# Attention backward for one query per head: uneven K loads, larger stores, a coarser last V load

## The chip, the core and the metric

The kernel runs on one core of a Trainium2 chip. The core has a matrix engine (PE), a vector engine (DVE), a scalar engine (ACT), GpSimd (POOL) and a sync engine (SP) that issues transfers; the transfers themselves are carried by 16 DMA engines, which move rows between the device memory (HBM, "dram" in the profile) and the on-chip memory with its 128 partitions. The metric is device time in microseconds (us); less is better. The kernel before takes 668.13 us (median of 3 runs, 668.04 to 668.19).

## The reference, cut to what matters

There are 32 heads, one query row per head, 8192 keys and values of 128 numbers each, all bf16. What is computed is the attention output and the gradients of q, k and v for a given output gradient.

```python
B, H, Sq, Skv, Dh = 1, 32, 1, 8192, 128

def _fwd_reference(q, k, v):
    scale = q.shape[-1] ** -0.5
    scores = jnp.einsum('bhqd,bhkd->bhqk', q, k) * scale
    attn = _softmax(scores, axis=-1)
    return jnp.einsum('bhqk,bhkd->bhqd', attn, v)

def reference(q, k, v, grad_out):
    _out, _vjp = jax.vjp(_fwd_reference, q, k, v)
    return (_out, *_vjp(grad_out))          # out, dq, dk, dv
```

Per head, K and V are 2 MB each and are read once; dk and dv are 2 MB each and are written once. Since there is one query row, dk is the outer product of the score gradient (ds, 8192 numbers) with the q row, and dv the outer product of the probabilities (p) with the output-gradient row. Over 32 heads that is 134 MB in and 134 MB out.

## The kernel before: the parts that the change touches

Each head's 8192 rows are laid out as 128 partitions of NT = 64 consecutive rows ("slots") of 256 bytes, so that a partition's share of one head is 16 KB in one piece in HBM and on chip. A quarter of a head is CH = 16 slots per partition.

```python
CH = 16
R = 4
K_BUFS = 3
V_BUFS = 2
NST = 2
...
    NT = S // P              # 64 slots per partition
    NCH = NT // CH           # 4 quarters
...
    def rows_of(x, h, c, parts):
        L = NT // parts
        return x[0, h].rearrange("(p n) d -> p n d", p=P)[:, c * L:(c + 1) * L, :]

    def slots(X, c, parts):
        L = NT // parts
        return X[:, c * L:(c + 1) * L, :]

    def load_k(h):
        Kt[h] = kpool.tile([P, NT, D], BF16, tag="K", name="Kt")
        parts = NCH if h == 0 else 1
        for c in range(parts):
            nc.sync.dma_start(slots(Kt[h], c, parts), rows_of(k, h, c, parts))

    def load_v(h):
        Vt[h] = vpool.tile([P, NT, D], BF16, tag="V", name="Vt")
        parts = NCH if h in (0, H - 1) else 1
        for c in range(parts):
            nc.sync.dma_start(slots(Vt[h], c, parts), rows_of(v, h, c, parts))
```

A gradient tile G (dk or dv of one head) is written by DVE in four quarters, and sent out when enough quarters are done: with NST = 2 a store of 1 MB after every second quarter, and in the last head a store of 0.5 MB after each.

```python
    def outer(h, which, r):
        x = st[h]
        if r == 0:
            x[which] = gpool.tile([P, NT, D], BF16, tag=which, name="G_" + which)
        G, dst = x[which], out_2 if which == "dk" else out_3
        ...
        nc.vector.tensor_tensor(
            slots(G, r, 4).rearrange("p n (a b) -> p n a b", b=R), ..., op=ALU.mult)
        parts = 4 if h == H - 1 else NST
        if r % (4 // parts) == 4 // parts - 1:
            c = r // (4 // parts)
            nc.sync.dma_start(rows_of(dst, h, c, parts), slots(G, c, parts))
```

The loop over heads overlaps the scores of head h with the gradients of head h - 1. In each iteration the transfers are issued, all by SP and in this order:

```python
    for h in range(H + 1):
        p_ = h - 1
        if h < H:
            ...                                   # k_blocks x4 (DVE transposes), k_scores (PE)
            if 0 < h < H - 1:
                load_v(h + 1)
        if h > 0:
            ds_of(p_); outer(p_, "dk", 0); dq_of(p_, 0)
        ...
            dq_of(p_, 1); outer(p_, "dk", 1)      # store: first half of dk
        if 0 < h and h + 2 < H:
            load_k(h + 2)
        ...                                       # softmax of head h, outer(p_, "dk", 2)
        if h > 0:
            outer(p_, "dk", 3)                    # store: second half of dk
        if h == H:
            break
        ...                                       # p, v_transposes (PE, ACT), contract, v_scores
        outer(h, "dv", 0); outer(h, "dv", 1)      # store: first half of dv
        outer(h, "dv", 2); outer(h, "dv", 3)      # store: second half of dv
```

So one iteration issues six transfers: V (2 MB), half of dk (1 MB), K (2 MB), half of dk, and two halves of dv. The build gives the transfers eight completion semaphores in turn: a transfer is issued only when the one eight places before it has landed.

Of the kernel before, what the change touches and what calls it, by code (L numbers as in the profile page):

```python
# [16 lines left out]
R = 4  # L17
K_BUFS = 3
V_BUFS = 2
NST = 2  # L20
QD = 32


@with_exitstack
def kernel(
# [11 lines left out]
    nc = tc.nc  # L37
    P = 128
    _, H, S, D = k.shape
    assert D == P and S % (P * CH) == 0 and H <= P  # L40
    NT = S // P
    NCH = NT // CH
    NQ = P // QD
    assert NCH == 4 and NQ == 4
    W = D // 2
    NB = W // QD
    scale = float(D) ** -0.5
# [13 lines left out]
    Kt, Vt, XK, XV, st = {}, {}, {}, {}, {}  # L61
# [8 lines that stand above are left out]

    def load_k(h):
        Kt[h] = kpool.tile([P, NT, D], BF16, tag="K", name="Kt")
        parts = NCH if h == 0 else 1
        for c in range(parts):
            nc.sync.dma_start(slots(Kt[h], c, parts), rows_of(k, h, c, parts))

    def load_v(h):
        Vt[h] = vpool.tile([P, NT, D], BF16, tag="V", name="Vt")
        parts = NCH if h in (0, H - 1) else 1
        for c in range(parts):  # L80
            nc.sync.dma_start(slots(Vt[h], c, parts), rows_of(v, h, c, parts))

    rows = consts.tile([H, 2, D], BF16)
    nc.sync.dma_start(rows[:, 0, :], q.rearrange("b h s d -> (b h s) d"))
    nc.sync.dma_start(rows[:, 1, :], grad_out.rearrange("b h s d -> (b h s) d"))
    load_k(0)
    load_v(0)
    load_k(1)
    load_v(1)

    ident = consts.tile([P, P], BF16)
# [6 lines left out]
    nc.vector.reduce_sum(in_quad[:], ident[:].rearrange("p (a i) -> p a i", a=NQ), axis=AX.X)  # L98
    lane = consts.tile([P, QD], F32)
    nc.vector.reduce_sum(lane[:], ident[:].rearrange("p (a i) -> p i a", a=NQ), axis=AX.X)  # L100
# [3 lines left out]
    for w in range(NB):  # L104
        for e2 in range(2):
            four = consts.tile([H, NQ, QD], BF16, tag=f"four{w}{e2}")
            nc.vector.tensor_copy(
                four[:], rows[:, 0, :].rearrange("h (w j e) -> h w e j", w=NB, e=2)[:, w, e2:e2 + 1, :]
                .to_broadcast([H, NQ, QD]))
            tp = psT.tile([P, CH, P], BF16, tag="T")  # L110
# [17 lines left out]
    def k_blocks(h, u):  # L128


        if u == 0:
            XK[h] = ktpool.tile([P, CH, NB, NCH, QD], F32, tag="XK", name="XK_sb")
        nc.vector.transpose(XK[h][:, :, :, u, :],  # L133
# [54 lines left out]
# [5 lines that stand above are left out]
        rep, row = x["ds"] if which == "dk" else x["p"], x["qd"][:, 0 if which == "dk" else 1, :]  # L193
        Q = NT // 4
        nc.vector.tensor_tensor(  # L195
            slots(G, r, 4).rearrange("p n (a b) -> p n a b", b=R),
            slots(rep, r, 4).unsqueeze(2).to_broadcast([P, Q, D // R, R]),
            row.rearrange("p (a b) -> p a b", b=R).unsqueeze(1).to_broadcast([P, Q, D // R, R]),
            op=ALU.mult)
        parts = 4 if h == H - 1 else NST  # L200
        if r % (4 // parts) == 4 // parts - 1:
            c = r // (4 // parts)
            nc.sync.dma_start(rows_of(dst, h, c, parts), slots(G, c, parts))
# [24 lines left out]
# [3 lines that stand above are left out]
            x = st[h] = {}  # L231
            for u in range(NCH):
                k_blocks(h, u)
            k_scores(h)
# [3 lines that stand above are left out]
            ds_of(p_)  # L238
            outer(p_, "dk", 0)
            dq_of(p_, 0)  # L240
# [3 lines left out]
        if h > 0:  # L244
            dq_of(p_, 1)
            outer(p_, "dk", 1)
        if 0 < h and h + 2 < H:
            load_k(h + 2)
# [9 lines left out]
        if h > 0:  # L258
            outer(p_, "dk", 2)
# [77 lines left out]
```

## Time and profile before

| | before |
|---|---|
| time, median of 3 | 668.13 us |
| span of the profiled execution | 667.0 us |
| PE busy | 516.8 us (77%) |
| DVE busy | 512.5 us (77%) |
| ACT busy | 182.1 us (27%) |
| share of the 16 DMA engines' time, data transfers | 97.0% |
| share of the 16 DMA engines' time, instruction fetches | 0.7% |
| read and written | 134.23 MB and 134.23 MB, 403 GB/s over the span |

The profile is of one execution. A busy share is averaged over the whole span. The line of DMA digits divides the span in 40 slices, each digit the mean busy share of the 16 DMA engines in tenths (9 is 90% or more), and the line under it gives the GB/s moved in each slice. The chain "that ended last" follows the end of the program back from releaser to releaser. Under the page lies the trace, which holds a record for each packet that a DMA engine moved (start, duration in ns, bytes) and for each of the up to 16 semaphore counts by which the DMA engines report that their share of a transfer has landed. A packet record does not name its DMA engine.

### The profile page before, as it was taken

How to read it: one execution, taken by the hardware profiler on the slowest of the kernel's cores; microseconds unless marked ns; L12 is line 12 of the kernel's file. 1: busy time of each engine (PE TensorE's matmuls, PEld its weight loads, DVE VectorE, ACT ScalarE, POOL GpSimd, SP SyncE). 2: the span in 40 equal slices, each digit the busy share in tenths (PEclk: the TensorE clock that was granted, in tenths of full speed). 3: DMA queues.
4: the chain of work that ended last, by engine and by line, in shares of the span. 5: the costliest groups of instructions: out<-in, count | busy, mean ns of one | idle time of the engine just before them, and what ended most of it. 6: DMA issues, size and time to landing. Idle time of an engine off the chain costs nothing.

```text
span 667.0 us, 23105 instructions
## 1 busy us (share of the span) xinstructions
PE 516.8 (77%) x10727; PEld 485.8 (73%) x10727; DVE 512.5 (77%) x658; ACT 182.1 (27%) x321; POOL 0.7 (0%) x6
## 2 busy tenths in 40 slices
PE   2887988888887777878779787787776888778881
PEld 1887878878877767877668676677766777677870
DVE  4797888888877797777877778777788776887762
ACT  0333323232323222232222322223312223223230
POOL 0000000000000000000000000000000000000000
PEclk9995556566565565555555655666557665555555
DMA  8999999999999999999999999999999999999783
GB/s 330 414 425 424 419 427 414 424 423 426 425 425 424 425 425 424 425 429 423 423 427 426 423 416 422 413 412 418 395 423 418 397 416 406 409 420 403 270 357 142
DMA packets 29807, 269.94 MB, mean 405 GB/s; under 512 B 3472, under 2 KB 3472, under 8 KB 6032
## 3 DMA queue, kind: packets, MB, share of 16 engines
q1 hardware_dynamic: 29712, 268.48, 97.0%
q8 instruction: 83, 1.36, 0.7%
q14 instruction: 12, 0.10, 0.0%
HBM read 134.23 MB, written 134.23 MB: 403 GB/s over the span
## 4 chain that ended last, share of the span: by engine, by line
DMA 75%; PE 17%; DVE 3%; ACT 2%; issue 1%; SPq 0%; ACTq 0%
DMA Kt<-in_k_dram 26%; DMA Vt<-in_v_dram 26%; DMA out_dram<-G_dv 23%; PE T_ps L168 7%; PE s_ps L145 2%; PE dp_ps L185 2%; PE m_ps L185 2%; PE dp_ps L180 1%; DVE XK_sb L133 1%; ACT XT_sb L170 1%; PE m_ps L255 1%; DVE G_dk L195 1%; PE m_ps L268 1%; PE s_ps L161 0%; ACT qd L211 0%
## 5 line engine op out<-in xcount | busy, mean ns | idle before, releaser
L168 PE MATMUL T_ps<-ident,Vt 128*128 128x128 bf16 x2048 | 228.7, 302 | 31.9 <-DMA Vt<-in_v_dram 31.9
L168 PEld LDWEIGHTS <-Vt 128*128 128x128 bf16 x2048 | 201.1, 142 | 33.8 <-DMA Vt<-in_v_dram 33.6
L133 DVE STREAM_TRANSPOSE XK_sb<-Kt 128x1024 f32<-128x1024 f32 x128 | 148.2, 1213 | 81.1 <-DMA Kt<-in_k_dram 81.1
L170 ACT COPY XT_sb<-T_ps 128x1024 f32<-128x1024 f32 x128 | 129.5, 1012 | 189.7 <-PE T_ps L168 189.7
L195 DVE TENSOR_TENSOR G_dk<-ds_rep,qd 128x2048 bf16<-128x2048 bf16 x128 | 155.7, 1219 | 1.1
L195 DVE TENSOR_TENSOR G_dv<-p_rep,qd 128x2048 bf16<-128x2048 bf16 x128 | 148.2, 1220 | 8.5 <-ACT p_rep L277 8.5
L180 PEld LDWEIGHTS <-XT_sb 128*128 128x128 bf16 x2048 | 74.7, 106 | 27.2 <-ACT XT_sb L170 27.2
L180 PE MATMUL dp_ps<-doT,XT_sb 128*128 128x1 bf16 x2048 | 73.6, 166 | 24.4 <-ACT XT_sb L170 24.4
L145 PE MATMUL s_ps<-q_blk,XK_sb 128*128 128x4 bf16 x2048 | 59.1, 168 | 23.2 <-DVE pdt L216 20.5
L145 PEld LDWEIGHTS <-XK_sb 128*128 128x128 bf16 x2048 | 56.5, 103 | 25.5 <-DVE pdt L216 22.3
L185 PE MATMUL dp_ps<-ds_rep,Kt 128*128 128x1 bf16 x2048 | 64.7, 165 | 6.6 <-issue 6.0
L185 PEld LDWEIGHTS <-Kt 128*128 128x128 bf16 x2048 | 59.9, 104 | 12.3 <-issue 12.3
L185 PEld LDWEIGHTS <-Vt 128*128 128x128 bf16 x2048 | 61.1, 105 | 0.0
L185 PE MATMUL m_ps<-p_rep,Vt 128*128 128x1 bf16 x2048 | 60.5, 166 | 0.0
L226 ACT COPY dq_all<-dp_ps 128x1 f32<-128x1 f32 x32 | 5.1, 159 | 173.9 <-PE dp_ps L185 173.9
L268 PEld LDWEIGHTS m_ps<-rs,ones_f 128*128 128x128 f32 x64 | 16.0, 310 | 48.6 <-ACT e L267 48.6
L268 PE MATMUL m_ps<-rs,ones_f 128*128 128x1 f32 x64 | 18.7, 360 | 39.2 <-ACT e L267 39.2
L264 DVE TENSOR_REDUCE nbias<-m_ps 128x1 f32<-128x128 f32 x32 | 9.3, 292 | 22.0 <-ACT qd L211 22.0
L255 PE MATMUL m_ps<-diag,ones_f 128*128 128x128 f32 x64 | 25.3, 499 | 0.7 <-DVE diag L253 0.7
L218 DVE SCALAR_TENSOR_TENSOR ds_rep<-dp_ps,pdt,p_s 128x256 bf16<-128x256 f32 x32 | 15.5, 484 | 12.0 <-PE dp_ps L180 9.6
L277 ACT ACTIVATE p_rep<-e,rinv 128x256 bf16<-128x256 f32 x32 | 16.2, 507 | 30.3 <-DVE rinv L275 30.3
L211 ACT CAST qd<-m_ps 128x256 bf16<-128x256 f32 x32 | 11.9, 372 | 42.4 <-PE m_ps L207 42.4
(40 smaller groups left out, 163.0 us busy)
## 6 DMA issues: line engine op xcount, KB each, us to landing
Kt<-in_k_dram SPq DMA_DIRECT2D x31, 2048.0 KB, 28.0
out_dram<-G_dv SPq DMA_DIRECT2D x62, 1024.0 KB, 25.8
out_dram<-G_dk SPq DMA_DIRECT2D x62, 1024.0 KB, 28.0
Vt<-in_v_dram SPq DMA_DIRECT2D x30, 2048.0 KB, 28.3
Vt<-in_v_dram SPq DMA_DIRECT2D x8, 512.0 KB, 13.8
Kt<-in_k_dram SPq DMA_DIRECT2D x4, 512.0 KB, 5.4
out_dram<-G_dv SPq DMA_DIRECT2D x4, 512.0 KB, 16.9
out_dram<-G_dk SPq DMA_DIRECT2D x4, 512.0 KB, 10.7
```

The lines of the kernel that those rows point to most:

```text
L133: nc.vector.transpose(XK[h][:, :, :, u, :], slots(Kt[h], u, NCH).rearrange("p g d -> p (g d)").bitcast(F32).rearrange("p (g w j) -> p g w ...
L145: nc.tensor.matmul(out[:, g, :], lhsT=cols[:, g, c // 2, c % 2], rhs=q_blk[:, h, c, :], start=(c == 0), stop=(c == 2 * NB - 1), skip_group ...
L168: nc.tensor.transpose(T_ps[:, i, :], Vt[h][:, c * CH + i, :], ident[:])
L170: nc.scalar.copy(X.rearrange("p c s -> p (c s)").bitcast(F32), T_ps.rearrange("p c s -> p (c s)").bitcast(F32))
L180: nc.tensor.matmul(st[h]["dp"][:, n:n + 1], lhsT=X[:, i, :], rhs=doT[:, h:h + 1], start=True, stop=True, skip_group_check=True)
L185: nc.tensor.matmul(out_col, lhsT=Xt[:, n, :], rhs=rep[:, n, 0:1], start=(n == 0), stop=(n == NT - 1), skip_group_check=True)
L195: nc.vector.tensor_tensor(slots(G, r, 4).rearrange("p n (a b) -> p n a b", b=R), slots(rep, r, 4).unsqueeze(2).to_broadcast([P, Q, D // R, ...
L211: nc.scalar.copy(x["qd"][:].rearrange("p a d -> p (a d)"), x["m"][:, 256:512])
L218: nc.vector.scalar_tensor_tensor(out=x["ds"][:], in0=x["dp"][:, 0:NT].unsqueeze(2).to_broadcast([P, NT, R]), scalar=pdt[:], in1=x["p_s"][: ...
L255: nc.tensor.matmul(x["m"][:, 128:256], lhsT=ones_f[:], rhs=diag[:], start=True, stop=True, skip_group_check=True)
L268: nc.tensor.matmul(x["m"][:, 0:1], lhsT=ones_f[:], rhs=rs[:], start=True, stop=True, skip_group_check=True)
L277: nc.scalar.activation(x["p"][:], e[:].unsqueeze(2).to_broadcast([P, NT, R]), ACT.Copy, scale=rinv[:])
```

## The change

Every K load but the first head's is split in three. The first part takes 59 of the 64 slots of every partition. The remaining 5 slots (LIGHT_SLOTS) go in two transfers: one for partitions 0 to 118, whose 119 partitions are divided over 7 DMA engines, 17 each, and one for the nine partitions left. The purpose is to let the first 7 DMA engines carry more of the K bytes than the others, since the engines do not come out equally loaded. To keep the number of transfers per head at six, with eight in flight, the stores are made 2 MB (NST = 1) in all heads but the first (1 MB) and the last (0.5 MB), and the last head's V load goes in halves instead of quarters.

```diff
-NST = 2
+NST = 1
 QD = 32
+LIGHT_SLOTS = 5
...
     def load_k(h):
         Kt[h] = kpool.tile([P, NT, D], BF16, tag="K", name="Kt")
-        parts = NCH if h == 0 else 1
-        for c in range(parts):
-            nc.sync.dma_start(slots(Kt[h], c, parts), rows_of(k, h, c, parts))
+        if h == 0:
+            for c in range(NCH):
+                nc.sync.dma_start(slots(Kt[h], c, NCH), rows_of(k, h, c, NCH))
+        else:
+            src = rows_of(k, h, 0, 1)
+            m = NT - LIGHT_SLOTS
+            for rng, cut in ((slice(0, P), slice(0, m)), (slice(0, 119), slice(m, NT)),
+                             (slice(119, P), slice(m, NT))):
+                nc.sync.dma_start(Kt[h][rng, cut, :], src[rng, cut, :])

     def load_v(h):
         Vt[h] = vpool.tile([P, NT, D], BF16, tag="V", name="Vt")
-        parts = NCH if h in (0, H - 1) else 1
+        parts = NCH if h == 0 else 2 if h == H - 1 else 1
...
-        parts = 4 if h == H - 1 else NST
+        parts = 4 if h == H - 1 else 2 if h == 0 else NST
```

No instruction of PE, DVE, ACT or POOL changes, and SP issues as many transfers as before.

## The prediction

> **What bounds the kernel now.** I read the lines of slices first, then stretches of the span, then the sync engine's waits, then the record of single packets and landings.
>
> ```profile
> DMA  8999999999999999999999999999999999999783
> GB/s 330 414 425 424 419 427 414 424 423 426 425 425 424 425 425 424 425 429 423 423 427 426 423 416 422 413 412 418 395 423 418 397 416 406 409 420 403 270 357 142
> ...
> q1 hardware_dynamic: 29712, 268.48, 97.0%
> q8 instruction: 83, 1.36, 0.7%
> ```
>
> The DMA engines are full in all but the last three slices, so bytes bound the kernel, not PE or DVE (77% each). The rate is flat at 424 GB/s to slice 23, then sags. By stretch (columns: window, length, busy us of PE, PEld, DVE, ACT, POOL, granted clock, DMA share, GB/s):
>
> ```profile
> 100.00:395.00 295.00, 240.18 (x4980) 225.92 (x4979) 236.21 (x299) 83.73 (x149) 0.00 (x0) 0.54 1.01 424
> 395.00:600.00 205.00, 156.82 (x3284) 146.93 (x3282) 157.19 (x199) 55.34 (x99) 0.00 (x0) 0.58 1.01 412
> ...
> 645.00:660.00 15.00, 6.00 (x137) 5.51 (x135) 5.63 (x8) 2.18 (x3) 0.00 (x0) 0.61 0.63 247
> 660.00:667.00 7.00, 0.00 (x0) 0.00 (x0) 0.00 (x0) 0.00 (x0) 0.00 (x0) 0.50 0.05 19
> ```
>
> In the last 7 us no compute engine works and the DMA share is 0.05, about one engine of 16: something still drains. SP's waits (us in total, times, longest) say that issue is held mostly by transfers that have not landed:
>
> ```profile
> SPq L203 <- DMA out_dram<-G_dk: 111.7, 52, 2.5
> SPq L203 <- DMA Kt<-in_k_dram: 110.8, 26, 5.2
> SPq L75 <- DMA Vt<-in_v_dram: 97.5, 23, 4.5
> ```
>
> A transfer has landed only when all its engines have reported. So I put each transfer's landings in order, and worked out this table from the trace's landing record. A row is one transfer; columns are the earliest, the ninth, the fifteenth and the last report, us from the span's start.
>
> ```
> transfer        first    9th   15th   last
> first 2 MB K    18.28  18.51  19.06  19.11
> a V load       117.00 118.56 120.96 122.45
> a V load       312.35 319.66 321.86 328.26
> a V load       390.50 399.18 401.48 411.14
> a V load       597.54 600.30 605.88 618.33
> last dk store  657.64 657.74 657.81 665.03
> ```
>
> Equal shares, unequal speed. Three groups appear. About seven engines stay together at the front. Eight fall back in steps of some 1.4 us, which fits the 83 instruction fetches of 16 KB being spread over those eight. One falls back steadily, 15.9 us by 328, until from about 400 us the leaders can get no further ahead (some 20 us) and are throttled to its pace: that is the sag to 412. At the end only its packets are left, of 309 to 389 ns where 309 is normal for 8 KB, until 664.6 us. This one engine never idles, so **its total is the kernel's time**.
>
> Its durations per transfer (100 to 380 us): V 4.88, K 4.90, stores of 1 MB 2.60, 2.63, 2.64 and 2.93. It is slow in stores alone. Between the transfers landing last at 19.11 and 618.33 lie 232 MB, 29 heads: 599.2 / 29 = **20.66 us a head**. A front engine needs 4.88 + 4.88 + 4 x 2.455 = **19.58**; the middle ones lose some 0.5 more, **20.1**.
>
> **What the Trainium skill says.** (1) "DMA: Bandwidth & Descriptors", section "Why a DMA increments its semaphore by 16 and not by 1": a transfer from SP is spread over the largest k up to 16 that divides the outermost count, on the lowest-numbered k engines. Thus 119 partitions give 7 and 9 give 9. Every full transfer here shows 16 landings; 7 and 9 no run shows yet. (2) Same page, "Latency and other measured facts": engines 7 and 15 are usually slower than the rest. The trace agrees that one is slow (20.66 against 19.58) but gives no number for it. If it is 7 or 15 it lies outside the first seven, and the change is aimed right. (3) Same page, "Why small descriptors are slow (HBM only)": a fixed cost on each packet. Here packets start every 155.3 ns at 4 KB, 306 at 8 KB and 608 at 16 KB, so 0.0368 ns a byte plus about 4.6 ns.
>
> **The change part by part**, per head.
>
> *K on the slow engine.* It keeps 59/64: 4.90 x 59/64 = 4.52. By the rule it also gets one of the nine odd rows of 1,280 bytes, 0.0368 x 1280 + 4.6 = 52 ns, and two more reports of 6 ns. 4.90 - 4.52 - 0.06 = 0.32 saved; times 31 K loads, **9.9 us**. All of it is on the path.
>
> *K on the first seven.* 4.88 x 59/64 = 4.50, plus 18 rows of 52 ns = 0.94, plus 0.01: 5.45, so 0.57 more. From 19.58 to 20.15.
>
> *Stores of 2 MB.* Two sets of 8 packets of 8 KB with two reports are 16 x 306 + 12 = 4,908 ns; eight of 16 KB with one are 8 x 608 + 6 = 4,870. 38 ns a store, two a head, 0.076; times 30 heads 2.3 us, on every engine. Against it: the first megabyte of a gradient is issued two DVE pieces (2.4 us) later. The queue is held by landings, not by DVE, so I count nothing.
>
> *Last V in halves.* The tail starts its transposes at 638 us when quarters had landed from 635.3 on; a half would have landed at 636.5. Nothing.
>
> *Sum.* Slow engine 20.66 - 0.32 - 0.08 = 20.26; first seven 20.15 - 0.08 = 20.07; middle 20.1 - 0.38 - 0.08 = 19.6. The slow one still sets the end, by a hair. 9.9 + 2.3 = 12.2 us off 668.1: **655.9**. The leaders are now the middle engines, ahead by 0.65 x 30 = 20 us at the end against the slow one, about the old limit, so throttling nearly vanishes; that alone shortens nothing, since the slow engine was never the one throttled. The tail: V of head 31 landed at 639.1 and the compute after it took until 654.7, while the slow engine had 10 MB (26 us) to drain. With the landing some 12 us earlier compute still ends sooner than the drain.
>
> **Rivals.** (a) *The first seven become the bound.* 18 rows of 1,280 bytes are a size the trace does not hold. If one costs 10 ns more than my line, that is 0.18 a head and 5.6 us, less the 0.19 margin: about 656; at 20 ns more, 661. For it: short rows from scattered places. Against: the 256-byte rows at the start lasted 15 to 18 ns, on the line. (b) *The slow engine's penalty in stores is per packet or per transfer.* Then larger stores halve its excess of about 1 us a head and the seven bind at 20.07: 0.59 x 31 = 18 off, about 650 to 654. Against it: with the engine alone, 644 to 651 us, long packets come while PE and ACT work on the last head, and 309 after, which looks like contention in time, not a cost per packet. (c) *The slow engine is among the first seven.* Then it gains 0.57 a head instead: about 683. Against: the constant's name and purpose, and point (2). (d) *The 8-in-flight limit bites.* Two of the eight are now tiny, so the window can shrink from 9 MB to 8 (some 19 us at 424 GB/s). If the queue starves the front engines, nothing is lost; if it starves the slow one too, perhaps 3 us.
>
> **Range and chances.** The sum gives 655.9; (a) and (d) push up, (b) down; I take 656.5. The range 652 to 662 holds (a) at 20 ns and part of (b). Faster by over 2% means under 654.8, which needs (b) or a better store gain: 0.29. Within 2%: 0.66. Slower by over 2% is (c): 0.05.
>
> **What would show it.** Right: the last landings of a transfer trail the first by much less at 300 us, with first seven and slow engine together behind and eight in front; GB/s stays near 424 into slice 33; the lone drain of the last 7 us is gone; 15,104-byte packets near 563 ns and 1,280-byte ones near 55. Wrong: 1,280-byte packets of 75 ns or more (a), 16 KB store packets on the last engine near 611 (b), a lone engine trailing further (c), new SP waits on DVE with DMA slices under 9 in the middle (d).

## The result and the profile after

| | before | after |
|---|---|---|
| time, median | 668.09 us | 706.55 us (704.09 to 707.6) |
| span of the profiled execution | 667.0 us | 705.8 us |
| ratio, 95% interval | | 1.0571 (1.0542 to 1.0601) |
| predicted | | 656.5, range 652 to 662 |

The change made the kernel 5.7% slower. First the lines of slices and of queues in the page of the changed kernel, which answer to the first lines shown of the kernel before:

```profile
DMA  8999999999999999999999999999999999999863
GB/s 339 403 422 422 424 424 420 423 415 416 410 412 402 391 394 392 397 405 385 380 408 376 391 377 378 403 376 390 372 372 400 366 384 361 393 392 350 348 250 136
...
q1 hardware_dynamic: 25248, 268.48, 93.5%
q8 instruction: 84, 1.38, 0.8%
```

The DMA digits look as before, but the rate leaves 424 GB/s in slice 9 already, where the kernel before held it to slice 23, and it falls further. The stretches say the same (columns as in the prediction; the last two numbers are the DMA share and the GB/s):

```profile
20.00:100.00 80.00, 69.39 (x1452) 66.02 (x1450) 68.48 (x86) 24.81 (x43) 0.00 (x0) 0.62 1.01 421
100.00:395.00 295.00, 219.72 (x4668) 206.83 (x4666) 221.59 (x280) 78.32 (x140) 0.00 (x0) 0.57 0.99 402
395.00:640.00 245.00, 177.16 (x3707) 166.33 (x3708) 175.37 (x222) 63.01 (x111) 0.00 (x0) 0.56 0.95 381
698.00:705.80 7.80, 0.00 (x0) 0.00 (x0) 0.00 (x0) 0.00 (x0) 0.00 (x0) 0.50 0.06 22
```

402 and 381 stand against 424 and 412 before (there to 600 us; over the same stretch, 395 to 600 us, it is 380 now). The lone drain is still there: in the last 7.8 us no compute engine works and the DMA share is 0.06, one engine of 16. SP waits on landings as before, only longer (us in total, times, longest; L84 is a K load, L90 a V load):

```profile
SPq L84 <- DMA out_dram<-G_dv: 121.1, 24, 5.7
SPq L84 <- DMA Kt<-in_k_dram: 111.9, 27, 5.2
SPq L84 <- DMA Vt<-in_v_dram: 104.7, 27, 4.9
SPq L90 <- DMA out_dram<-G_dk: 100.2, 24, 4.7
```

Then the order of landings, worked out from the trace's landing record with the zero of the prediction's table (which lies 0.7 us after the span's start):

```
transfer        first    9th   15th   last
first K, part 1 17.93  18.22  18.77  18.84
a V load       114.63 117.63 124.60 125.68
a V load       302.65 303.70 315.19 322.94
a V load       389.80 390.18 400.05 411.36
a V load       589.68 589.90 591.07 610.85
last dk store  696.70 696.82 696.90 703.86
```

One engine ends alone again, and it is 20 us behind the first at some 200 us, where the kernel before needed some 400. Which engine it is, the small transfer tells. A transfer of 119 partitions brought 7 reports and one of 9 brought 9, as the rule of the Trainium skill ("DMA: Bandwidth & Descriptors", "Why a DMA increments its semaphore by 16 and not by 1") has it. The seven reports of one 119-partition transfer in the middle came at

```
462.01 462.03 462.05 462.09 466.12 468.45 483.33
```

So the engine that trails by 20 us is one of the seven that were meant to relieve it.

### The profile page after: what moved, and what is told of

It is laid out like the page before. It is cut to its first block, busy times and chain, and to the rows that moved or that the text cites. A ratio compares the mean times of both kernels' runs of the same rounds, so it can differ in the third digit from the quotient of the medians.

```text
span 705.8 us, 23108 instructions
## 1 busy us (share of the span) xinstructions
PE 510.9 (72%) x10727; PEld 480.0 (68%) x10727; DVE 511.2 (72%) x658; ACT 182.2 (26%) x321; POOL 0.7 (0%) x6
## 4 chain that ended last, share of the span: by engine, by line
DMA 79%; PE 14%; DVE 2%; ACT 2%; issue 1%; SPq 0%; ACTq 0%
DMA Vt<-in_v_dram 31%; DMA Kt<-in_k_dram 25%; DMA out_dram<-G_dk 23%; PE T_ps L177 6%; PE m_ps L194 2%; PE s_ps L154 1%; PE dp_ps L189 1%; PE dp_ps L194 1%; ACT XT_sb L179 1%; DVE XK_sb L142 1%; DVE G_dk L204 1%; PE m_ps L264 1%; PE m_ps L277 0%; ACT e L276 0%; PE s_ps L170 0%
## 5 line engine op out<-in xcount | busy, mean ns | idle before, releaser
L177 PE MATMUL T_ps<-ident,Vt 128*128 128x128 bf16 x2048 | 225.5, 299 | 78.1 <-DMA Vt<-in_v_dram 78.1
L177 PEld LDWEIGHTS <-Vt 128*128 128x128 bf16 x2048 | 198.0, 140 | 80.2 <-DMA Vt<-in_v_dram 80.2
L194 PEld LDWEIGHTS <-Vt 128*128 128x128 bf16 x2048 | 61.1, 105 | 0.0
L154 PE MATMUL s_ps<-q_blk,XK_sb 128*128 128x4 bf16 x2048 | 57.6, 167 | 2.6 <-DVE XK_sb L142 2.6
```

The costliest lines, as they stand in the source:

```text
L154: nc.tensor.matmul(out[:, g, :], lhsT=cols[:, g, c // 2, c % 2], rhs=q_blk[:, h, c, :], start=(c == 0), stop=(c == 2 * NB - 1), skip_group ...
L177: nc.tensor.transpose(T_ps[:, i, :], Vt[h][:, c * CH + i, :], ident[:])
L194: nc.tensor.matmul(out_col, lhsT=Xt[:, n, :], rhs=rep[:, n, 0:1], start=(n == 0), stop=(n == NT - 1), skip_group_check=True)
```

## The experiments

Where nothing else is said a time is the median of four runs, with its ratio to the kernel before on the same chip. "Slow engine" is the one whose reports come last; its durations are taken from last report to last report. A single packet's duration is worked out from the trace's packet records, which name no engine.

**Which engine is slow.** The kernel before with a probe:

```diff
             if 0 < h < H - 1:
                 load_v(h + 1)
+            if 12 <= h < 28:
+                n = h - 11
+                nc.sync.dma_start(probe[0:n, :], rows_of(k, 0, 0, 1)[0:n, 0, :])
```

> The kernel before, with one tiny extra load per head in heads 12 to 27: head h loads one 256-byte row into each of n = h - 11 partitions of a spare tile, so n = 1 to 16. If a transfer of n partitions runs on the n lowest engines, the report counts give n, and the last report of probe n is late as soon as the slow engine is among the first n. Theory A (the slow engine is one of the first seven): the last report trails the first by 15 to 20 us from some n of 7 or less on. Theory B (the slow engine is the eighth or later, as predicted): below n = 8 the trail is under 10 us, and jumps at 8 or above. Time within 3 us of 668 in both.

668.58 us (one run). The probes' reports, in us after the first report of the V load issued just ahead of them:

```
n=1   0.3
n=2   0.3  1.0
n=3   0.3  0.4  1.7
n=4   0.3  0.4  1.7  2.0
n=5   0.4  0.5  1.7  2.0 17.3
n=6   0.4  0.5  1.8  2.0  9.7 18.3
n=7   0.3  0.3  1.6  2.2  8.7 10.1 18.2
n=8   0.2  0.2  0.3  1.1  1.7  9.4  9.5 18.0
n=9   0.2  0.4  0.5  0.7  1.7  1.8  9.0  9.3 18.3
```

Each line adds one engine to those above. The first four are at the front, the fifth trails by 17 us, the sixth and seventh by 9, the eighth and ninth are at the front. So the slow engine is the fifth, and the sixth and seventh, by their lag, are two of the eight middle ones. Three of the first seven were among the laggards. The same probe put into the changed kernel (other chip, one run, 703.08 us) has its jump at the same place:

> The changed kernel with the probes of n = 1 to 16 partitions in heads 12 to 27. Theory A: the probes' last report jumps to some 20 us behind at n = 5, as in the kernel before, so that the slow engine is the fifth on another chip or in another run too; the others of the first seven stand in between. If the jump is at another n of 7 or less, the slow place is not fixed; at 8 or more, theory A is wrong for the changed kernel.

```
n=4   0.2  1.1  4.2  6.4
n=5   0.3  0.7  2.7  5.0 20.0
n=7   0.4  0.7  2.2  3.7  8.3  9.6 20.3
n=9   0.2  0.4  1.0  1.0  1.7  2.3  7.2  7.3 19.8
```

**The parts alone.** Stores of 2 MB without the K split:

```diff
-NST = 2
+NST = 1
...
-        parts = 4 if h == H - 1 else NST
+        parts = 4 if h == H - 1 else 2 if h == 0 else NST
```

> Only the 2 MB stores, K and last V as before. Theory A (the loss is the K split on the slow engine): 664 to 668, since the slow engine's stores per head went from 10.84 to 10.7 us in the changed kernel. Rival C (the loss is in the larger stores, which are issued later and hold the queue): 685 or more.

671.63 us, 1.0055 (1.0040 to 1.0070): a little slower, not a little faster. And the K split with stores of 1 MB and the last V in quarters:

```diff
 (in the changed kernel)
-NST = 1
+NST = 2
-        parts = NCH if h == 0 else 2 if h == H - 1 else 1
+        parts = NCH if h in (0, H - 1) else 1
```

> Only the K split, stores of 1 MB and last V in quarters as before, so eight transfers a head. Theory A: 705 to 713, the slow engine's K load costs 6.2 to 6.6 us a head instead of 4.9. Rival C (the stores are the loss): under 680.

703.98 us, 1.0543 (1.0528 to 1.0559). Nearly the whole loss is the K split.

**The five slots spread evenly.**

```diff
 (in the changed kernel)
-            for rng, cut in ((slice(0, P), slice(0, m)), (slice(0, 119), slice(m, NT)),
-                             (slice(119, P), slice(m, NT))):
+            for rng, cut in ((slice(0, P), slice(0, m)), (slice(0, P // 2), slice(m, NT)),
+                             (slice(P // 2, P), slice(m, NT))):
```

> The changed kernel, but the 5 slots go in two halves of 64 partitions each, over all 16 engines: as many transfers, as many short rows in all, 8 for each engine instead of 18, 1 or 0. Theory A with cheap rows (52 ns): 666. Theory A with rows at the 71 to 92 ns that the slow engine showed, and a cost of about 0.15 us per extra transfer: 675 to 685. Rival D (splitting off short rows costs the same wherever they go, through the shrunken window of eight transfers): as slow as the changed kernel, 700 or more.

685.76 us, 1.0260 (1.0243 to 1.0277). The uneven share is worth 21 us of the loss, but the even one still loses 14 us against the stores alone, although every engine carries exactly the bytes that it carries there. From report to report a transfer of four rows took the slow engine 0.281 us from 100 to 395 us and 0.326 from 400 to 600 us. That is not the rows' own time. The first of the two equal transfers took 0.36 and 0.44, the second 0.21 in both stretches, which is 50 to 51 ns a row after 6 ns for the report; and a 1,280-byte packet lasts 55 ns in the median here, 62 in the mean. So the first small report comes late after its rows, and most of the loss is not in the rows themselves: a head's K load as a whole took 5.17 and 5.94 us against 4.91 and 5.28 with the stores alone, and eight rows of 52 ns with their two reports would add only 0.04.

**Lifting K off the slow engine.** Two kernels that move whole 16 KB rows in every third head, to the first four engines or to the first five:

```diff
 (in the kernel before, at the start of load_k after the tile)
+        if h % 3 == 2:
+            src = rows_of(k, h, 0, 1)
+            for lo, hi in ((0, 112), (112, 116), (116, 120), (120, 124), (124, 128)):
+                nc.sync.dma_start(Kt[h][lo:hi, :, :], src[lo:hi, :, :])
+            return
 (or, for the first five)
+            for lo, hi in ((0, 112), (112, 117), (117, 122), (122, 127), (127, 128)):
```

> The kernel before, but in every third head (ten heads) K comes as one load of 112 partitions and four loads of 4 partitions, whole rows of 16 KB: the 12 engines from the fifth on carry 7 rows instead of 8, the first four 11. Theory A (the fifth engine is the slow one and sets the end): 10 x 0.61 = 6 us less, 661 to 664; the first four go from 19.6 to 20.2 us a head and do not bind. Theory B (the slow engine is among the first four, or differs from chip to chip): 3 rows more on it, 10 x 1.83 us, 686. Theory E (any split of a K load costs the slow engine some 0.3 us): 664 to 667.

> The pair of the lift-4 kernel: the same number of transfers and whole rows, but the 16 partitions go as three loads of 5 partitions and one of 1, so the first five engines get 3 rows each and the slow fifth carries 10 rows instead of 8 in ten heads. Theory A: 10 x 2 x 0.61 = 12 us more, 678 to 682. Theory B (position of the slow engine does not matter, or it lies beyond the fifth): 661 to 664 as in the pair.

690.24 us, 1.0356 (1.0316 to 1.0395), and 721.37 us, 1.0797 (1.0771 to 1.0822). The pair differs in the direction of theory A: giving the fifth engine more rows instead of fewer costs 31 us (18 were expected). But lifting, which should have gained 6 us, lost 22. The page of the lift-4 kernel shows where (GB/s by slice):

```profile
GB/s 333 332 425 424 419 368 424 425 384 398 427 422 376 403 426 392 324 403 425 362 398 422 429 345 376 427 426 349 395 427 375 363 426 423 347 377 421 422 421 261
```

Every third to fourth slice the rate drops to some 325 to 385 and returns to 425, about as often as a head whose K load is cut by partitions comes round (three heads are some 64 us, a slice is 17). Something in such a cut slows the transfers themselves.

The short rows moved to the first four engines, with 5 slots and with 3:

```diff
 (in the changed kernel; LIGHT_SLOTS = 5 or 3)
-            ... (slice(0, 119), slice(m, NT)), (slice(119, P), slice(m, NT)) ...
+            ... (slice(0, 124), slice(m, NT)), (slice(124, P), slice(m, NT)) ...
```

> The changed kernel with one thing different: the 5 slots go as 124 and 4 partitions instead of 119 and 9, so on the first four engines only, 32 short rows each, none on the slow fifth. Theory A with rows of 52 ns on a fast engine: the four need 20.8 us a head, the slow one 20.4, so 670 to 676 against 706. Theory D (short rows or the small transfers cost the kernel wherever they go): 700 or more.

> As the first-four kernel with 5 slots, but with 3 slots. Theory A: the four need 20.3 us a head, the slow engine 20.4 to 20.6, so 658 to 668. Theory D: 690 or more.

712.34 us, 1.0654 (1.0628 to 1.0679), and 681.91 us, 1.0209 (1.0191 to 1.0227). Both miss theory A's numbers by far. With 5 slots the four engines that report last need 21.1 to 22.1 us a head from 100 to 395 us, not 20.8, and one alone trails by 20 us at the end; their 31 short rows took 1.96 to 2.27 us between reports, and a 1,280-byte packet 65 ns in the mean. So theory A, the bytes on the slow engine alone, fell.

**Cutting by partitions against cutting by slots.** A new theory, F, which no record here can show directly: when a transfer has all 128 partitions, each engine writes to partitions that no other engine of that transfer shares a port with; any other partition count breaks this. It rests on what the Trainium skill says of the ports ("SBUF — State Buffer", section "Door 1: The DMA port swizzle": bandwidth depends on how many of 16 ports the partitions reach, and partitions 32 apart share one). The plainest test is one K load in two transfers of 1 MB, cut either way, on equal engines with equal bytes:

```diff
 (in the kernel before)
+        if h > 0:
+            src = rows_of(k, h, 0, 1)
+            for lo, hi in ((0, 64), (64, 128)):
+                nc.sync.dma_start(Kt[h][lo:hi, :, :], src[lo:hi, :, :])
+            return
 (or, the control)
-        parts = NCH if h == 0 else 1
+        parts = NCH if h == 0 else 2
```

> The kernel before, but each K load in two transfers of 64 partitions, whole rows of 16 KB, over all 16 engines, equal bytes for each. Theory F: 64 partitions reach half of the ports, two engines share one, a K load takes up to twice its 4.9 us: 690 to 820. Theory A and D (only the slow engine's rows, or only short rows, cost): 667 to 671.

> Control for the half-partition kernel: each K load in two transfers of 1 MB as well, but cut by slots, so that each has all 128 partitions and rows of 8 KB. Theory F, A and D: 667 to 671. If it is slow, the number of transfers is what costs.

Cut by partitions 836.3 us (826 to 845), 1.2384 (1.2354 to 1.2415); by slots 673.37 us, 1.0078 (1.0063 to 1.0093). The ratio of the kernel cut by partitions is taken from its two faster runs alone, 826 and 829 us (827 below), while its page is of the run of 845. Lines of that page: GB/s by slice; DVE's transposes of K (busy us, mean ns, idle us before them and for what); the issues (count, KB each, median us to landing):

```profile
GB/s 283 284 331 350 369 363 338 355 342 303 337 316 350 325 335 312 273 340 328 315 280 340 345 329 303 265 355 338 295 274 299 344 310 320 318 338 318 301 366 214
...
L138 DVE STREAM_TRANSPOSE XK_sb<-Kt 128x1024 f32<-128x1024 f32 x128 | 148.2, 1214 | 251.4 <-DMA Kt<-in_k_dram 251.4
...
Kt<-in_k_dram SPq DMA_DIRECT2D x62, 1024.0 KB, 31.0
...
Vt<-in_v_dram SPq DMA_DIRECT2D x30, 2048.0 KB, 34.2
```

The same lines of the page of the kernel cut by slots:

```profile
GB/s 329 420 417 421 424 424 423 424 422 423 423 424 424 423 423 422 424 422 424 419 408 408 415 411 417 411 414 410 405 417 413 402 394 399 406 411 393 273 372 143
...
L133 DVE STREAM_TRANSPOSE XK_sb<-Kt 128x1024 f32<-128x1024 f32 x128 | 151.0, 1221 | 52.8 <-DMA Kt<-in_k_dram 50.1
...
Kt<-in_k_dram SPq DMA_DIRECT2D x62, 1024.0 KB, 23.2
...
Vt<-in_v_dram SPq DMA_DIRECT2D x30, 2048.0 KB, 25.6
```

328 GB/s from 100 to 395 us against 421, and DVE waits five times as long for K. The packets show the kind of loss: cut by partitions, load packets of 16 KB have a median of 994 ns and an upper quartile of 1,241, twice the 611 that is normal (in the kernel cut by slots the 16 KB packets, all of them V, keep 611 for median and upper quartile). The 8 KB packets of the stores keep their 309. V, which is not cut, suffers too: 8.35 us from last report to last report instead of 4.87. So what is slowed is loads, cut or not, and by a factor near two in the slowest quarter of their packets. Whether it is their writing on chip, as theory F has it, or their reading of HBM, no run separates: the cut changes which engine takes which piece on both sides. A third kernel has the lift-4 cut in every head, without its lift:

```diff
-            for lo, hi in ((0, 64), (64, 128)):
+            for lo, hi in ((0, 112), (112, 128)):
```

> Each K load as 112 partitions and 16 partitions, whole rows, all 16 engines in both, 7 rows and 1 row each: equal bytes, no short rows, nothing lifted. It is the lift-4 kernel's cut without its lift, in every head instead of every third. Theory F: the mapping of engines to partitions is broken for the whole load, 690 or more. Theory A: 667 to 671.

780 to 822 us in four runs. Every engine has its 8 whole rows; the partitions that an engine gets are others, and there is one more transfer a load, which cost 5 us when it was cut by slots.

**Short rows with all 128 partitions.**

```diff
 (in the changed kernel)
-            m = NT - LIGHT_SLOTS
-            for rng, cut in ((slice(0, P), slice(0, m)), (slice(0, 119), slice(m, NT)),
-                             (slice(119, P), slice(m, NT))):
+            m = NT - 2 * LIGHT_SLOTS
+            for rng, cut in ((slice(0, P), slice(0, m)), (slice(0, P), slice(m, m + LIGHT_SLOTS)),
+                             (slice(0, P), slice(m + LIGHT_SLOTS, NT))):
```

> The changed kernel, but the three K transfers all take all 128 partitions: 54 slots, 5 and 5. Every engine gets 16 short rows of 1,280 bytes, nearly the 18 that the first seven had. Theory F (what costs is that a transfer of fewer than 128 partitions gives engines rows of partitions whose on-chip port another engine is using): 16 rows x 5 ns of fixed cost is nothing, so near the stores-only kernel, 670 to 676. Theory D (short rows are slow in themselves, some 56 ns more each, as the even split showed): 16 x 0.056 = 0.9 us a head, 698 or more.

679.18 us, 1.0165 (1.0150 to 1.0180), 3 us above what theory F allowed and far under theory D. Sixteen short rows on every engine cost 7.6 us against the stores alone. On the slow engine such a row took 54 ns between reports from 100 to 395 us (62 later), the 52 ns of the prediction's line or little more. Half as many rows, in transfers of 112 and 16 partitions:

```diff
 (in the changed kernel)
-            ... (slice(0, 119), slice(m, NT)), (slice(119, P), slice(m, NT)) ...
+            ... (slice(0, 112), slice(m, NT)), (slice(112, P), slice(m, NT)) ...
```

> The changed kernel, but the 5 slots go as 112 and 16 partitions over all 16 engines: 8 short rows for each engine, half of those in the kernel whose three K transfers all have 128 partitions (679.2). Bytes and rows alone: 675. Theory F: slower than 679 in spite of half the short rows, about the 686 of the 64 and 64 cut.

681.23 us, 1.0199 (1.0162 to 1.0235). That lies between the two expectations, and its interval reaches down to the kernel with 16 rows: the time does not decide. Nor does the duration of a row. Between reports the seven rows took 0.48 to 0.54 us, 68 to 76 ns each, but the single row that follows took 0.20. In one head, at some 442 us, the slow engine's eight short packets are the only ones for more than 1.5 us: they start 52 ns apart, as with 128 partitions, and 58 across the report, while the reports are 0.52 and 0.20 us apart. Last, the same bytes on the same engines with other partitions:

```diff
 (in the changed kernel)
-            ... (slice(0, 119), slice(m, NT)), (slice(119, P), slice(m, NT)) ...
+            ... (slice(9, P), slice(m, NT)), (slice(0, 9), slice(m, NT)) ...
```

> The changed kernel with the two small transfers' partitions moved: 119 partitions from 9 to 127 on the first seven engines, and partitions 0 to 8 on the first nine. Every engine carries exactly the rows and bytes that it carries in the changed kernel; only which partitions they belong to differs. Theory A alone (bytes on the slow engine): 704 to 708, as the changed kernel. Theory F (rows meeting other engines at the ports): a different time, by 3 us or more, in either direction.

704.99 us, 1.0556 (1.0539 to 1.0572), no different from the changed kernel. Theory F's guess of 3 us missed: which partitions the seven are given matters little. Between reports its rows took 74 to 77 ns; the packets have a median of 55 ns and a mean of 60.

## Why the prediction was wrong

**What bounds the kernel: right.** One DMA engine never idles and its total is the time, after as before: the lone drain at the end, and the sync engine issuing each large K part at least 8 us, from 100 us on at least 18 us, before the slow engine had finished what lay ahead of it. Rival (d), the limit of eight starving the slow engine, is out with that.

**The step that failed: "If it is 7 or 15 it lies outside the first seven, and the change is aimed right."** The trace before could not tell which engine was slow, and I took the place from a general remark and from the name of a constant. The probes show it to be the fifth. The place in the Trainium skill behind that remark ("DMA: Bandwidth & Descriptors", "Latency and other measured facts") counts from 0, so its 7 and 15 are the eighth and the sixteenth, and the measurement here does not agree with it. The same row calls its suspected cause special to transfers issued another way (SWDGE, from GpSimd); here SP issues them all, and the prediction left that out. So the change put 17 more short rows a head on the engine that sets the end: where the prediction has its K load fall by 0.32 us a head, it rose from 4.90 to between 6.2 and 6.6. That is rival (c), to which I gave 0.05.

**The short rows: a row's usual cost right, what small transfers do to the loads beside them left out.** Rival (c) with the line of 52 ns made "about 683", not 706. The slow engine's account per head, from 100 to 395 us and from 400 to 600 us, between reports:

| us per head | predicted | measured |
|---|---|---|
| K, 59 slots | 4.52 | 4.80, 4.84 |
| the 119-partition transfer | 0 | 1.21, 1.57 |
| the 9-partition transfer and both stores | 10.78 | 10.87, 10.99 |
| V | 4.88 | 5.00, 4.88 |
| sum | 20.2 | 21.9, 22.3 |

Seventeen rows at 52 ns and a report would be 0.89; between reports they took 71 to 92 ns a row. Over 31 K loads and with the means of the two stretches: 0.89 x 31 = 28 us for rows that were to go elsewhere, 0.50 x 31 = 15 for the rest of that transfer, 0.30 x 31 = 9 for the large part of K, and the 2.3 us hoped for from the stores. 655.9 + 54 = 710, against 706.6. This is rough: the rises in V and in the stores are left out, before 100 us the 119-partition transfer still took only about 0.8, and by an estimate some 0.15 of the 0.50 is the late first report (a single row took 0.207 between reports where 0.058 is enough), which the transfers after it give back.

Rival (a) had named its own sign, 1,280-byte packets of 75 ns or more. The usual packet does not show it: from 100 to 600 us the median is 55 ns and the mean 61, against 55 and 58 where all transfers have 128 partitions, and the 15,104-byte packets have a median of 565 ns, as forecast. But 8% of the short packets last 75 ns or more, against 2% there. The slow engine's own are not named; its 1.21 and 1.57 us less 0.15 leave 62 to 83 ns a row, an estimate. What the cut does go with is slow large packets beside the short ones. Of the changed kernel's 15,104-byte packets from 100 to 395 us, 17% took over 1.15 times their median of 567 ns when a short row of another engine started during them, and 2% when none did. In the kernel whose three K transfers all have 128 partitions it is under 1% of the 13,824-byte packets either way. So a part of the 0.3 more on the large K part goes with the small transfers of other engines. Not all of it: in the kernel with the larger stores alone a K load also went from 4.91 to 5.28 from 400 us on, where nothing is cut. How the 23 us above rival (c) divide is not settled.

That cutting whole rows by partitions slows loads is shown (827 against 673); that it is the sharing of a port is theory F's account, built on that page, and fits the doubled packets, but no record names a partition or a port, and a cause on the HBM side is not ruled out.

**Stores of 2 MB: sign wrong.** Expected 2.3 us less, measured 3.7 more. The front engines did gain (4.85 instead of 4.90 for 2 MB), the slow engine did not: 10.81 to 10.95 us a head against 10.84 to 10.92 before. Rival (b), a penalty by packet or transfer, is out. From 400 to 600 us its whole head took 21.11 us where it had been 20.74, which over the rest of the run is about the 3.7 us. By reports the K load stands out (5.28), but before the change a store reports ahead of it and now a load, so that the single transfers do not compare; the cause is open.

**Last V in halves:** not tried alone, so its share, if it has one, is open.

No kernel here beats the one before. One that takes work off the fifth engine without cutting by partitions was not found: by the rule for the number of engines, a transfer on fewer than 16 needs a partition count other than 128.

## What to carry to other kernels

When bytes bound a kernel, order the landing reports of single transfers: they show whether the engines keep step, and a probe of n partitions for n = 1, 2, 3 ... shows which engine does not. Do that before aiming a change at particular engines. And where a large load is to be cut, cut it along its rows rather than by partitions: with the same bytes on the same engines the kernel took 673 us one way and 827 the other.

## What the runs showed of the hardware that was not expected

- The slow DMA engine was the fifth in both probed runs, on two chips; in the kernel before it is slow in stores (2.6 to 2.9 us for 1 MB against 2.45) and hardly in loads (4.88 to 4.94 us for 2 MB against 4.86 to 4.88).
- A K load cut into two transfers of 64 partitions, or of 112 and 16, brings the whole kernel to some 780 to 845 us, and slows the uncut V loads with it, while store packets keep their 309 ns.
- A packet of 1,280 bytes lasts 55 ns in the median whether its transfer has 128 partitions or 64, 112 or 119 (in the mean 58 against 60 to 62). It is the large load packets beside it that are slow more often with fewer partitions: 17% against 2% with 119, under 1% either way with 128.
- The time between two reports is not the time of the rows when a transfer is small: on the slow engine a transfer of one 1,280-byte row took 0.20 us from report to report, and one of four rows that followed another small one 0.21.
- A second transfer per K load, cut by slots, cost 5.3 us over 31 loads (673.37 against 668.04), 0.17 us each.
